# Denominator sums of blocks one to seven folded to one term on VectorE, and half of the first norm's transposes moved to DMA

## The chip, the cores and the metric

The kernel runs on one core of a Trainium2 chip. The metric is the device time of one execution in microseconds (us); lower is better. Before the change the median of three runs is 1134.34 us (1134.11 to 1134.49).

## What is computed

One transformer layer with conditioned norms: 2048 tokens of width 1024, multi-query attention with 32 heads of width 32 over one shared K and V, and a gated feed-forward network (FFN) of width 3584. All arrays are bf16.

```
mod = (silu(c) @ w_mod): sa, ca, ga, sb, cb, gb          # six rows of 1024
h = layernorm(x) * (1 + ca) + sa
q, k, v = h @ wq, h @ wk, h @ wv                          # 32 heads share k and v
p = softmax(q k^T / sqrt(32));  o = p v
x = x + ga * (o @ wo)
h = layernorm(x) * (1 + cb) + sb
out = x + gb * ((silu(h @ w1) * (h @ w3)) @ w2)
```

## The kernel before, in words

**Tiles.** Tokens are cut into 16 tiles of 128 and 8 blocks of 256. The first norm handles one token tile at a time (`lnt1`, L656): VectorE (DVE) computes statistics, GpSimd (POOL) the reciprocal root, and the normalized tile XN is made on ScalarE (ACT) for tiles 0 to 7 and on VectorE for tiles 8 to 15. XN has three slots, used in turn (tile number modulo 3: two halves of XNB and a piece of PS). TensorE (PE) then transposes the tile in eight 128x128 steps into a PSUM bank, and ACT or VectorE copies it into HT, the transposed activations. From HT come K (`k_proj`, L757, two token tiles a call, its result copied to KT by VectorE or ACT), V (`v_proj`, L772) and Q (`q_proj`, L787).

**Attention.** A unit is one block of 256 queries and four heads: 8 blocks times 8 groups make 64 units. A unit has 8 chunks of 256 keys, so there are 512 chunks in a fixed order. For a chunk, `s_exp` (L850) issues 8 score matmuls (named S<-QT,KT in the profile) and two exponentials on ACT, which write the chunk into one of ten slots of U. Chunk j of a unit needs KT of token tiles 2j and 2j+1. `av` (L881) multiplies the unit's 8 chunks by V on PE (64 matmuls, PB<-U,V) and forms the softmax denominators: VectorE adds chunks pairwise into slots of PS (`pairs`, L870, PS<-U), folds these slots further (PS<-PS), and PE sums what is left over the keys by multiplying with ones (PB<-PS,ONES, four matmuls per slot left). How far VectorE folds is `level(u)` (L878): for units 0 to 7 (block zero) level 2 leaves four slots, for later units level 3 leaves two. VectorE then inverts the denominators and scales the output into QT.

**The rest of a block.** `wo` (L946) applies the output projection, the second norm and its transposes (for blocks 1 to 6 by a DMA transpose issued from SyncE, SP; named QT<-XNB). `slab` (L1005) is the first half of the FFN, 14 slabs a block, each with a tanh on ACT; `quarter` (L1042) is the second half. The FFN of block n runs beside the attention of block n+1, so that of block 7 stands alone at the end. Weights stream from HBM through DMAs that SP issues.

**What sets the order.** All instructions are recorded as a graph; `Placer` (L187) places them one by one on the engines by planned durations, ready times and urgencies, and each engine then runs its list strictly in that order, waiting at semaphores. Score matmuls have the highest urgency; the other PE work fills the gaps. PLAN (L115) holds weights for every 16 chunks, which shift urgencies. All instructions are played through one helper, so that the profile gives L22 for nearly all of them, and tile names tell them apart. PE works in modes: score matmuls on row groups, full matrices, and column groups for values and denominators.

**The start.** SP issues the loads of x, of two slices of w_mod and of wq, then waits until the last part of wq has landed and issues WO and the first chunks of w_mod for the other fields (W2S<-in_w_mod; `mod_chunk`, L809).

Of the kernel before, what the change touches and what calls it, by code (L numbers as in the profile page):

```python
# [42 lines left out]
class Graph:  # L43
# [63 lines left out]
    def alias(self, new, old):  # L107
# [5 lines left out]


PLAN = [  # L115
    (0.2, 0.03, 0.0, 0, 1.4,
     {"q/pe": -9, "slab/act": -80, "wo/dve": -71, "ln/pe": -112, "ln/act": 31, "k/pe": 3, "k/dve": 33}),
    (0.0, 0.12, 0.2, 1, 0.2,
     {"av/pe": -2, "q/pe": -9, "pair/dve": -2, "av/dve": -33, "slab/act": -18, "ln/pe": -57, "ln/act": 23}),
    (0.0, 0.16, 0.02, 0, 0.7, {"wo/pe": 106, "q/pe": -45, "q/dve": -74, "ln/pe": -118, "ln/dve": 4, "mod/pe": -24}),  # L120
    (0.0, 0.16, 0.02, 0, 0.7, {"wo/pe": 106, "q/pe": -45, "q/dve": -74, "ln/pe": -118, "ln/dve": 4, "mod/pe": -24}),
    (0.2, 0.24, 0.2, 1, 0.6, {"q/pe": 47, "mc/pe": 46, "ln/act": -12, "k/pe": 22}),
    (0.0, 0.12, 0.2, 0, 1.8,
     {"wo/pe": -44, "quarter/pe": 47, "q/pe": 33, "mc/pe": 36, "pair/dve": -14, "wo/dve": -1, "ln/act": -12,
      "k/pe": 22}),
    (0.0, 0.11, 0.2, 1, 1.5, {"q/pe": 47, "mc/pe": 46, "av/dve": 6, "ln/act": -12, "k/pe": 22}),
    (0.0, 0.11, 0.2, 1, 1.9, {"q/pe": -13, "mc/pe": 46, "av/dve": 4, "ln/act": -12, "k/pe": 22}),
    (0.0, 0.11, 0.2, 0, 3.4, {"wo/pe": 35, "an/dve": 55, "slab/dve": 1}),
    (0.0, 0.11, 0.2, 1, 1.4, {"av/dve": -11, "an/dve": 55, "slab/dve": 1, "q/dve": 9}),
    (0.0, 0.11, 0.1, 0, 2.4,  # L130
     {"wo/pe": 14, "slab/pe": 12, "quarter/pe": 3, "q/pe": -6, "av/dve": 18, "an/dve": 69, "slab/act": -1,
      "quarter/dve": -7}),
    (0.0, 0.11, 0.05, 0, 2.4, {"slab/act": 6, "wo/dve": 53}),
    (0.0, 0.11, 0.2, 0, 2.9, {"wo/pe": 46, "an/dve": 55, "slab/dve": -89, "q/dve": 67}),
    (0.0, 0.11, 0.2, 1, 1.3, {"wo/pe": -13, "pair/dve": 6, "an/dve": 55, "slab/dve": -89, "q/dve": 67}),
    (0.0, 0.11, 0.1, 1, 2.7,
     {"slab/pe": -132, "q/pe": 47, "mc/pe": 46, "pair/dve": -13, "av/dve": 23, "slab/dve": -39, "slab/act": -20,
      "quarter/dve": -47, "ln/act": -12, "k/pe": 22}),
    (0.0, 0.11, 0.1, 1, 2.3,
     {"slab/pe": -132, "q/pe": 47, "mc/pe": 46, "pair/dve": -13, "av/dve": -84, "slab/act": -20,  # L140
      "quarter/dve": -47, "ln/act": -12, "k/pe": 22}),
    (0.0, 0.11, 0.2, 1, 4.1,
     {"wo/pe": 138, "slab/pe": -132, "quarter/pe": 13, "q/pe": 47, "mc/pe": 46, "pair/dve": -13, "av/dve": -83,
      "slab/dve": -39, "slab/act": -20, "quarter/dve": -47, "ln/act": -12, "k/pe": 22}),
    (0.0, 0.11, 0.2, 1, 1.3,
     {"slab/pe": -124, "q/pe": 47, "mc/pe": 46, "pair/dve": -24, "av/dve": -89, "an/dve": -26, "slab/dve": -39,
      "slab/act": -20, "ln/act": -12, "k/pe": 22}),
    (0.0, 0.11, 0.05, 1, 3.7,
     {"wo/pe": -5, "quarter/pe": 48, "pair/dve": -3, "av/dve": -2, "slab/act": -7, "wo/dve": 20}),
    (0.0, 0.11, 0.05, 1, 3.7,  # L150
     {"wo/pe": -5, "quarter/pe": 48, "pair/dve": -3, "av/dve": -2, "slab/act": -7, "wo/dve": 20}),
    (0.0, 0.11, 0.2, 1, 2.6,
     {"wo/pe": 112, "slab/pe": -124, "quarter/pe": 26, "q/pe": 20, "mc/pe": 46, "pair/dve": 13, "av/dve": -89,
      "an/dve": -26, "slab/dve": -39, "slab/act": -20, "quarter/dve": 35, "wo/dve": -2, "ln/act": -12,
      "k/pe": 22}),
    (0.0, 0.11, 0.2, 1, 1.3,
     {"slab/pe": -124, "quarter/pe": 26, "q/pe": 52, "mc/pe": 46, "pair/dve": 13, "av/dve": -72, "an/dve": -26,
      "slab/dve": -39, "slab/act": -20, "quarter/dve": 35, "wo/dve": -6, "ln/act": -12, "k/pe": 22}),
    (0.0, 0.11, 0.05, 1, 2.6,
     {"slab/pe": -124, "quarter/pe": 26, "q/pe": 20, "mc/pe": 46, "av/dve": -89, "slab/dve": -39,  # L160
      "slab/act": -20, "quarter/dve": 35, "ln/act": -12, "k/pe": 22}),
    (0.0, 0.11, 0.05, 1, 1.4,
     {"slab/pe": -124, "quarter/pe": 26, "q/pe": 20, "mc/pe": 5, "av/dve": -89, "slab/act": -20,
      "quarter/dve": 35, "ln/act": -12, "k/pe": 22}),
    (0.0, 0.11, 0.2, 0, 1.6, {"wo/pe": 74, "pair/dve": 40, "av/dve": -2, "an/dve": 55, "slab/dve": -102, "q/dve": 6}),
    (0.0, 0.11, 0.2, 1, 1.4, {"wo/pe": -13, "pair/dve": 40, "av/dve": -2, "an/dve": 55, "slab/dve": -88}),
    (0.0, 0.11, 0.05, 1, 1.9,
     {"slab/pe": -124, "quarter/pe": -21, "q/pe": 20, "mc/pe": 46, "pair/dve": 43, "av/dve": -89,
      "slab/dve": -39, "slab/act": -20, "quarter/dve": 35, "ln/act": -12, "k/pe": 22}),
    (0.0, 0.11, 0.05, 1, 1.9,  # L170
     {"slab/pe": -124, "quarter/pe": -21, "q/pe": 20, "mc/pe": 46, "pair/dve": 43, "av/dve": -89,
      "slab/act": -20, "quarter/dve": 35, "ln/act": -12, "k/pe": 22}),
    (0.0, 0.11, 0.2, 0, 3.4, {"wo/pe": 61, "q/pe": -20, "pair/dve": 3, "slab/dve": -23, "wo/dve": 33}),
    (0.0, 0.11, 0.2, 1, 1.4, {"wo/pe": -5, "quarter/pe": 48, "pair/dve": -20, "av/dve": -27, "slab/act": -7}),
    (0.0, 0.11, 0.05, 0, 2.1,
     {"slab/pe": -124, "quarter/pe": -21, "q/pe": 20, "mc/pe": 46, "pair/dve": 43, "av/dve": -89,
      "slab/dve": -39, "slab/act": -20, "quarter/dve": 35, "q/dve": -75, "ln/act": -12, "k/pe": 22}),
    (0.0, 0.11, 0.05, 0, 4.0,
     {"slab/pe": -124, "quarter/pe": -21, "q/pe": 20, "mc/pe": 46, "pair/dve": 43, "av/dve": -89,
      "slab/act": -20, "quarter/dve": 35, "q/dve": -75, "ln/act": -12, "k/pe": 22}),  # L180
    (0.0, 0.11, 0.2, 0, 3.7,
     {"wo/pe": -4, "slab/pe": -43, "q/pe": 20, "mc/pe": 46, "pair/dve": 43, "av/dve": 55, "slab/dve": -39,
      "slab/act": -20, "quarter/dve": 35, "q/dve": -75, "ln/act": -12, "k/pe": 22}),
]


class Placer:  # L187
# [121 lines left out]
    def commit(self, n, e, k, start):  # L309
        eng, fn, dur = n.alts[k]  # L310
        e = eng
        s = n.sess
        if s is not None and s.bank is None:
            bt, b = self.bank_for(n)
            s.bank = b
            s.prev = self.bank_of[b][1]
            self.bank_of[b] = None
            for p in s.prev:
                n.preds.setdefault(p, False)
        n.eng = e  # L320
        if e == "sp" or n.dma is not None:
            self.t[e] = start + dur
            self.bw = max(self.bw, start + 2.6) + n.nbytes / n.bw
            n.fin = self.bw + 0.5
        else:
            if e == "dve" and n.tag in ("pair", "av"):
                self.lock = start + dur
            if e == "pool" and self.lock > start:
                dur = max(dur, self.lock - start + (0.43 if dur > 0.5 else 0.1))
            self.t[e] = start + dur  # L330
            n.fin = start + dur + n.post + self.SEM
        if e == "pe":
            if s is not None and n.mode == "F":
                s.fill = any(not x.done and x is not n and x.alts[0][0] == "pe" for x in s.nodes)
                if s.fill:
                    self.fills.add(s)
                else:
                    self.fills.discard(s)
            if n.mode == "S":
                self.step += 1  # L340
            self.mode = n.mode
            if n.mode != "S":
                self.run_of = n.mode
            else:
                self.t_s = self.t["pe"]
        n.done = True
        if s is not None:
            s.left -= 1
            if s.left == 0:
                users = [x for x in s.nodes if x.eng != "pe"] or [s.nodes[-1]]  # L350
                self.bank_of[s.bank] = (max(x.fin for x in users), tuple(users))
        self.emit(n, e, fn)
        self.free_pending()
# [90 lines left out]
def build(nc, x_in, wq_in, wk_in, wv_in, wo_in, w1_in, w3_in, w2_in, c_in, wmod_in, out, S, D, F):  # L444
# [89 lines left out]
    def xkey(tt):  # L534
        return [("X", tt // 2, tt % 2, q) for q in range(4)] if tt < 6 else [("XS", tt)]
# [120 lines left out]
    def lnt1(tt, vt):  # L656
# [10 lines left out]
               reads=xkey(tt) + [("RS", tt), ("NB", tt)], writes=[("XN", slot)], vt=vt)  # L667
        else:
            ln_norm(xap, tt, xkey(tt), slot, vt)
        static = tt < 6  # L670
        s = None if static else Sess()
        bk = [("S", tt)] if static else [("sess", id(s), tt)]
# [203 lines left out]
           writes=[("PS", (c + k) % NP) for k in range(2)], vt=c + 101.0, post=0.08)  # L876

    def level(u):  # L878
        return 2 if u < 8 else 3

    def av(u):  # L881
        G.tag = "av"
# [342 lines left out]
```

## Time and profile before

| what | value |
|---|---|
| median of the runs | 1134.34 us |
| the profiled execution's own time | 1134.47 us |
| its span (first to last instruction) | 1132.6 us |
| PE busy | 1113.1 us (98%) |
| ACT busy | 1026.0 us (91%) |
| DVE busy | 951.9 us (84%) |
| DMA, mean over the span | 185 GB/s |
| clock granted to PE | 1.00 |
| first score matmul | 30.13 us |
| last score matmul | 1033.80 us |

Times in the trace are microseconds from the start of the span; what lies around the span is 1.9 us of the execution's own time. A matmul's end is modelled, so a busy PE is not PE at its peak. An engine's busy time is the union of its instructions. In the lines of waits the engine that waits stands to the left of the arrow.

### The profile page before, as it was taken

The numbers are of one execution on the slowest core, as the hardware profiler recorded it, in microseconds if no ns is written. First come the engines' busy times: TensorE is split into PE (matmuls) and PEld (weight loads), VectorE is DVE, ScalarE is ACT, GpSimd is POOL, SyncE is SP. The second block draws the span as 40 slices with busy tenths as digits, with TensorE's granted clock in tenths as the row PEclk, the third lists the DMA queues.
The fourth block names the chain that finished last, engine by engine and source line by source line (L and its number), as shares of the span: only waits on it lengthen the run. The fifth ranks groups of instructions, "written<-read, shape, count | busy, mean of one in ns | idle before, by whom it ended". The sixth has DMA issues, their size and how long they took to land.

```text
span 1132.6 us, 34805 instructions
## 1 busy us (share of the span) xinstructions
PE 1113.1 (98%) x15600; PEld 754.6 (67%) x15600; DVE 951.9 (84%) x1544; ACT 1026.0 (91%) x1165; POOL 53.8 (5%) x95
## 2 busy tenths in 40 slices
PE   7999999999999999999999999999999999999998
PEld 6643546666577656776567756776577657766887
DVE  7888899989988888888988998888988988888442
ACT  6999999999999999999999999999999999996110
POOL 5100000000100001000100000000100000000000
PEclk9999999999999999999999999999999999999999
DMA  9500379665596667766596658765696559667793
GB/s 344 184 2 1 114 225 242 186 196 151 129 263 194 173 166 209 208 191 165 141 262 192 174 148 237 196 193 142 173 248 195 160 146 238 190 185 209 217 296 116
DMA packets 374292, 209.47 MB, mean 185 GB/s; under 512 B 17536, under 2 KB 365952, under 8 KB 374144
## 3 DMA queue, kind: packets, MB, share of 16 engines
q1 hardware_dynamic: 373712, 207.11, 65.8%
q8 instruction: 123, 2.02, 0.8%
q14 instruction: 25, 0.20, 0.1%
q10 hardware_dynamic: 432, 0.13, 0.0%
HBM read 199.89 MB, written 4.19 MB: 180 GB/s over the span
## 4 chain that ended last, share of the span: by engine, by line
PE 63%; ACT 31%; DVE 4%; DMA 1%; issue 0%; POOL 0%; SPq 0%; DVEq 0%
PE PB L22 47%; ACT U L22 30%; PE S L22 16%; DVE PS L22 2%; DMA W<-in_A_wq_dram 1%; ACT HT L22 1%; DVE HT L22 1%; DVE RB L22 0%; SPq L22 0%; DVE ST L22 0%; DVE W L22 0%; ACT XNB L22 0%; POOL PS L22 0%; DVE XNB L22 0%; POOL RS L22 0%
## 5 line engine op out<-in xcount | busy, mean ns | idle before, releaser
L22 ACT ACTIVATE U<-S 128x1024 bf16<-128x1024 f32 x1024 | 964.3, 1111 | 9.0 <-PE S L22 8.8
L22 DVE TENSOR_TENSOR PS<-U 128x2048 bf16<-128x2048 bf16 x256 | 309.7, 1214 | 11.7 <-ACT U L22 10.3
L22 DVE TENSOR_TENSOR PS<-PS 128x1024 bf16<-128x1024 bf16 x368 | 249.5, 684 | 4.7
L22 PE MATMUL PB<-QT,W 128*128 128x256 bf16 x1856 | 229.6, 273 | 0.0
L22 PE MATMUL S<-QT,KT 32*128 32x256 bf16 x4096 | 203.5, 273 | 6.0 <-ACT U L22 4.0
L22 PEld LDWEIGHTS PB<-QT,W 128*128 128x128 bf16 x1856 | 170.3, 98 | 46.6 <-issue 28.3
L22 PE MATMUL PB<-W2S,HT 128*128 128x256 bf16 x1512 | 189.1, 273 | 0.0
L22 PEld LDWEIGHTS PB<-W2S,HT 128*128 128x128 bf16 x1512 | 137.5, 98 | 42.4 <-issue 26.4
L22 PEld LDWEIGHTS S<-QT,KT 32*128 32x128 bf16 x4096 | 60.8, 92 | 132.7 <-ACT U L22 118.7
L22 PE MATMUL PB<-U,V 128*32 128x256 bf16 x4032 | 123.5, 273 | 0.0
L22 PE MATMUL PB<-QT,HT 128*128 128x256 bf16 x960 | 119.9, 273 | 0.0
L22 PEld LDWEIGHTS PB<-U,V 128*32 128x32 bf16 x4032 | 100.8, 97 | 18.8 <-issue 7.0
L22 ACT ACTIVATE HT<-PB 128x512 bf16<-128x512 f32 (+1 forms) x110 | 77.6, 707 | 32.0 <-PE PB L22 31.8
L22 PEld LDWEIGHTS PB<-QT,HT 128*128 128x128 bf16 x960 | 88.2, 98 | 23.7 <-issue 14.1
L22 PE MATMUL PB<-HT,W 128*128 128x256 bf16 (+1 forms) x576 | 101.8, 318 | 1.0 <-DVE HT L22 0.6
L22 DVE SCALAR_TENSOR_TENSOR HT<-HT,PB 128x512 bf16<-128x512 bf16 x102 | 69.4, 681 | 34.2 <-ACT HT L22 33.4
L22 DVE TENSOR_TENSOR HT<-HT,PB 128x512 bf16<-128x512 bf16 x102 | 69.5, 681 | 19.2 <-PE PB L22 18.5
L22 PEld LDWEIGHTS PB<-HT,W 128*128 128x128 bf16 x576 | 49.9, 97 | 38.1 <-issue 15.2
L22 DVE STREAM_TRANSPOSE RB<-PB 128x256 f32<-128x256 f32 x63 | 28.2, 448 | 38.7 <-PE PB L22 38.5
L22 PE MATMUL PB<-WO,QT 128*128 128x512 bf16 x232 | 57.3, 381 | 0.0
L22 POOL TENSOR_SCALAR RS<-MV 128x1 f32<-128x1 f32 x32 | 10.5, 329 | 969.9 <-DVE MV L22 966.9
L22 ACT ACTIVATE HT<-S 128x512 bf16<-128x512 f32 (+1 forms) x15 | 10.9, 736 | 30.5 <-PE S L22 30.5
(115 smaller groups left out, 675.2 us busy)
## 6 DMA issues: line engine op xcount, KB each, us to landing
W<-in_B_w_dram SPq DMA_DIRECT2D x150, 512.0 KB, 4.8
W2S<-in_B_w_dram SPq DMA_DIRECT2D x28, 1792.0 KB, 8.6
HT<-in_B_w_dram SPq DMA_DIRECT2D x74, 512.0 KB, 4.8
W2S<-in_w_mod_dram SPq DMA_DIRECT2D x8, 1024.0 KB, 7.2
X<-in_A_x_dram SPq DMA_DIRECT2D x8, 512.0 KB, 7.0
out_dram<-X SPq DMA_DIRECT2D x7, 512.0 KB, 9.1
U<-in_B_w_dram SPq DMA_DIRECT2D x1, 3584.0 KB, 13.5
W2S<-in_B_w_dram SPq DMA_DIRECT2D x1, 3584.0 KB, 15.2
```

What stands on the lines that cost most here:

```text
L22: return getattr(e, call[0])(*call[1], **call[2])
```

## The change

Three edits. `level(u)` becomes 4 for units 8 to 63: VectorE adds the last two slots of a unit as well, and PE multiplies one slot by ones in place of two. For token tiles 8 to 15 the first norm's transposition becomes a DMA transpose from XN to HT, issued by SP; its eight PE transposes and the copy out of PSUM go. The planner is given a duration of its own for these transposes, which doesn't pass through its queue of DMA bytes. And PLAN is replaced as a whole, so that the order changes on every engine.

```
-        return 2 if u < 8 else 3
+        return 2 if u < 8 else 4
...
         else:
             ln_norm(xap, tt, xkey(tt), slot, vt)
+        if tt >= 8:
+            o = op("sp", lambda: [lambda e: e.dma_start_transpose(HT[:, :, tt * P:(tt + 1) * P], XN[slot])], 0.5,
+                   reads=[("XN", slot)], writes=[("HT", cc, tt) for cc in range(NC)], vt=vt, dma=("HTL", slot), nbytes=1 << 18)
+            o.bw = -262144.0 / 1.0 * 1.0
+            return
         static = tt < 6
...
-            self.bw = max(self.bw, start + 2.6) + n.nbytes / n.bw
-            n.fin = self.bw + 0.5
+            if n.bw < 0:
+                n.fin = start + 2.6 - n.nbytes / n.bw + 0.5
+            else:
+                self.bw = max(self.bw, start + 2.6) + n.nbytes / n.bw
+                n.fin = self.bw + 0.5
...
-    (0.2, 0.03, 0.0, 0, 1.4,
-     {"q/pe": -9, "slab/act": -80, "wo/dve": -71, "ln/pe": -112, "ln/act": 31, "k/pe": 3, "k/dve": 33}),
...
+    (0.0, 0.12, 0.2, 0, 2.6,
+     {"slab/pe": -44, "q/pe": -9, "mc/pe": 25, "slab/dve": -38, "slab/act": -18, "wo/dve": -95, "ln/pe": -112,
+      "ln/act": 172, "k/dve": 33, "mod/pe": 109}),
...
```

In the built program the matmuls with ones fall from 576 to 352. On SP the transposes of tiles 8, 9 and 10 stand behind the last load of x; then come the two loads of WO, the transpose of tile 11, two loads of w_mod chunks, and the transposes of tiles 12 to 15. On VectorE the norm of tile 11 waits until the transpose of tile 8 has freed its slot, that of tile 12 waits for the transpose of tile 9, and that of tile 15 for that of tile 12. On PE the K projections of token tiles 8 to 15 (four calls of `k_proj`) stand ahead of score groups 2, 3, 6 and 7 in the list and wait for the transposes.

More of the change, by code (lines that the diff above doesn't have):

```diff
@@ L115 @@
 PLAN = [
-    (0.2, 0.03, 0.0, 0, 1.4,
-     {"q/pe": -9, "slab/act": -80, "wo/dve": -71, "ln/pe": -112, "ln/act": 31, "k/pe": 3, "k/dve": 33}),
[L118 to L121, printed above, removed]
@@ L122 @@
-    (0.2, 0.24, 0.2, 1, 0.6, {"q/pe": 47, "mc/pe": 46, "ln/act": -12, "k/pe": 22}),
-    (0.0, 0.12, 0.2, 0, 1.8,
-     {"wo/pe": -44, "quarter/pe": 47, "q/pe": 33, "mc/pe": 36, "pair/dve": -14, "wo/dve": -1, "ln/act": -12,
-      "k/pe": 22}),
-    (0.0, 0.11, 0.2, 1, 1.5, {"q/pe": 47, "mc/pe": 46, "av/dve": 6, "ln/act": -12, "k/pe": 22}),
-    (0.0, 0.11, 0.2, 1, 1.9, {"q/pe": -13, "mc/pe": 46, "av/dve": 4, "ln/act": -12, "k/pe": 22}),
-    (0.0, 0.11, 0.2, 0, 3.4, {"wo/pe": 35, "an/dve": 55, "slab/dve": 1}),
@@ L129 @@
[L129 to L139, printed above, removed]
+    (0.0, 0.12, 0.2, 0, 2.6,
+     {"slab/pe": -44, "q/pe": -9, "mc/pe": 25, "slab/dve": -38, "slab/act": -18, "wo/dve": -95, "ln/pe": -112,
+      "ln/act": 172, "k/dve": 33, "mod/pe": 109}),
+    (0.0, 0.15, 0.2, 1, 0.7,
+     {"wo/pe": 16, "slab/pe": -44, "q/pe": -17, "mc/pe": 25, "pair/dve": 8, "slab/dve": -38, "slab/act": -18,
+      "wo/dve": -95, "ln/pe": -112, "ln/dve": -122, "ln/act": 172, "k/dve": 33, "mod/pe": 109, "kb/pe": 8}),
@@ new lines @@
+    (0.0, 0.15, 0.1, 0, 0.7, {"wo/pe": 106, "q/pe": -78, "q/dve": -74, "ln/pe": -118, "ln/dve": 4, "mod/pe": -24}),
+    (0.2, 0.17, 0.1, 0, 0.8, {"mc/pe": 22, "av/dve": 1, "an/dve": -68, "q/dve": -18, "k/dve": 75, "kb/pe": 16}),
+    (0.0, 0.23, 0.2, 0, 1.3,
+     {"quarter/pe": -49, "mc/pe": 22, "av/dve": 106, "slab/dve": 9, "quarter/dve": 26, "q/dve": -28,
+      "kb/pe": -47}),
+    (0.0, 0.13, 0.2, 1, 3.3,
+     {"av/pe": -14, "wo/pe": -44, "quarter/pe": -31, "q/pe": 28, "mc/pe": -6, "pair/dve": -2, "an/dve": -18,
+      "wo/dve": 2, "q/dve": 16, "ln/act": -12, "k/pe": 22}),
@@ new lines @@
+    (0.0, 0.14, 0.2, 1, 3.3,
+     {"av/pe": -14, "wo/pe": -44, "quarter/pe": 47, "q/pe": 28, "pair/dve": -2, "an/dve": -18, "wo/dve": 2,
+      "q/dve": 16, "ln/act": -12, "k/pe": 22}),
+    (0.0, 0.11, 0.2, 1, 3.8,
+     {"av/pe": 11, "wo/pe": -44, "quarter/pe": 47, "pair/dve": -49, "av/dve": -48, "wo/dve": 2, "ln/act": -12,
+      "k/pe": 22}),
+    (0.0, 0.16, 0.2, 1, 0.5,
+     {"av/pe": 11, "wo/pe": -44, "quarter/pe": 47, "pair/dve": -2, "av/dve": -48, "an/dve": -9, "wo/dve": 2,
+      "q/dve": -59, "ln/act": -12, "k/pe": 22}),
@@ new lines @@
+    (0.0, 0.16, 0.2, 1, 0.5,
+     {"av/pe": 11, "wo/pe": -44, "quarter/pe": 47, "pair/dve": -2, "av/dve": -48, "an/dve": -9, "wo/dve": 2,
+      "q/dve": -59, "ln/act": -12, "k/pe": 22}),
+    (0.0, 0.11, 0.2, 0, 1.1, {"wo/pe": -17, "slab/dve": -19, "wo/dve": 53}),
+    (0.0, 0.11, 0.2, 1, 1.6, {"q/pe": -13, "mc/pe": 46, "av/dve": 40, "ln/act": -12, "k/pe": 22}),
+    (0.0, 0.12, 0.2, 0, 0.7,
+     {"slab/pe": -25, "quarter/pe": 11, "q/pe": -15, "mc/pe": -14, "av/dve": 40, "ln/act": -12, "k/pe": 22}),
@@ new lines @@
+    (0.0, 0.11, 0.2, 1, 1.5, {"av/dve": -8, "an/dve": 29, "slab/act": 6, "wo/dve": 53}),
+    (0.0, 0.11, 0.2, 1, 1.5, {"av/dve": -8, "an/dve": 29, "slab/act": 6, "wo/dve": 53}),
+    (0.0, 0.11, 0.2, 1, 1.5, {"av/dve": -8, "an/dve": 29, "slab/act": 6, "wo/dve": 53}),
+    (0.0, 0.11, 0.2, 1, 1.5, {"av/dve": -8, "an/dve": 29, "slab/act": 6, "wo/dve": 53}),
+    (0.0, 0.11, 0.2, 1, 1.5, {"av/dve": -8, "an/dve": 29, "slab/act": 6, "wo/dve": 53}),
+    (0.0, 0.11, 0.2, 0, 1.4,
+     {"mc/pe": 46, "av/dve": 35, "slab/dve": -88, "slab/act": 7, "q/dve": -25, "ln/act": -12, "k/pe": 22}),
@@ L140 @@
+    (0.0, 0.11, 0.2, 0, 1.4,
+     {"mc/pe": 46, "av/dve": 35, "slab/dve": -88, "slab/act": 7, "q/dve": -25, "ln/act": -12, "k/pe": 22}),
+    (0.0, 0.11, 0.2, 1, 2.3,
      {"slab/pe": -132, "q/pe": 47, "mc/pe": 46, "pair/dve": -13, "av/dve": -84, "slab/act": -20,
       "quarter/dve": -47, "ln/act": -12, "k/pe": 22}),
-    (0.0, 0.11, 0.2, 1, 4.1,
-     {"wo/pe": 138, "slab/pe": -132, "quarter/pe": 13, "q/pe": 47, "mc/pe": 46, "pair/dve": -13, "av/dve": -83,
-      "slab/dve": -39, "slab/act": -20, "quarter/dve": -47, "ln/act": -12, "k/pe": 22}),
@@ L145 @@
[L145 to L180, printed above, removed]
@@ L181 @@
-    (0.0, 0.11, 0.2, 0, 3.7,
-     {"wo/pe": -4, "slab/pe": -43, "q/pe": 20, "mc/pe": 46, "pair/dve": 43, "av/dve": 55, "slab/dve": -39,
-      "slab/act": -20, "quarter/dve": 35, "q/dve": -75, "ln/act": -12, "k/pe": 22}),
+    (0.0, 0.11, 0.2, 1, 1.4,
+     {"slab/pe": -132, "quarter/pe": 13, "q/pe": 47, "mc/pe": 46, "av/dve": 3, "slab/dve": -39,
+      "quarter/dve": -47, "wo/dve": -48, "q/dve": -7, "ln/act": -12, "k/pe": 22}),
+    (0.0, 0.11, 0.2, 1, 1.4,
+     {"slab/pe": -132, "quarter/pe": 13, "q/pe": 47, "mc/pe": 46, "av/dve": 3, "slab/dve": -39,
+      "quarter/dve": -47, "wo/dve": -48, "q/dve": -7, "ln/act": -12, "k/pe": 22}),
@@ new lines @@
+    (0.0, 0.11, 0.2, 1, 1.4,
+     {"slab/pe": -132, "quarter/pe": 13, "q/pe": 47, "mc/pe": 46, "av/dve": 3, "slab/dve": -39,
+      "quarter/dve": -47, "wo/dve": -48, "q/dve": -7, "ln/act": -12, "k/pe": 22}),
+    (0.0, 0.11, 0.2, 1, 1.4,
+     {"slab/pe": -132, "quarter/pe": 13, "q/pe": 47, "mc/pe": 46, "av/dve": 3, "slab/dve": -39,
+      "quarter/dve": -47, "wo/dve": -48, "q/dve": -7, "ln/act": -12, "k/pe": 22}),
+    (0.0, 0.11, 0.2, 1, 1.4,
+     {"slab/pe": -132, "quarter/pe": 13, "q/pe": 47, "mc/pe": 46, "av/dve": 3, "slab/dve": -39,
+      "quarter/dve": -47, "wo/dve": -48, "q/dve": -7, "ln/act": -12, "k/pe": 22}),
@@ new lines @@
+    (0.0, 0.11, 0.2, 1, 1.4,
+     {"slab/pe": -132, "quarter/pe": 13, "q/pe": 47, "mc/pe": 46, "av/dve": 3, "slab/dve": -39,
+      "quarter/dve": -47, "wo/dve": -48, "q/dve": -7, "ln/act": -12, "k/pe": 22}),
+    (0.0, 0.11, 0.2, 1, 1.4,
+     {"slab/pe": -132, "quarter/pe": 13, "q/pe": 47, "mc/pe": 46, "av/dve": 3, "slab/dve": -39,
+      "quarter/dve": -47, "wo/dve": -48, "q/dve": -7, "ln/act": -12, "k/pe": 22}),
+    (0.0, 0.11, 0.2, 1, 1.4,
+     {"slab/pe": -132, "quarter/pe": 13, "q/pe": 47, "mc/pe": 46, "av/dve": 3, "slab/dve": -39,
+      "quarter/dve": -47, "wo/dve": -48, "q/dve": -7, "ln/act": -12, "k/pe": 22}),
@@ new lines @@
+    (0.0, 0.11, 0.2, 1, 1.4,
+     {"slab/pe": -132, "quarter/pe": 13, "q/pe": 47, "mc/pe": 46, "av/dve": 3, "slab/dve": -39,
+      "quarter/dve": -47, "wo/dve": -48, "q/dve": -7, "ln/act": -12, "k/pe": 22}),
+    (0.0, 0.11, 0.2, 1, 1.4,
+     {"slab/pe": -132, "quarter/pe": 13, "q/pe": 47, "mc/pe": 46, "av/dve": 3, "slab/dve": -39,
+      "quarter/dve": -47, "wo/dve": -48, "q/dve": -7, "ln/act": -12, "k/pe": 22}),
+    (0.0, 0.11, 0.2, 0, 4.0,
+     {"av/pe": 6, "slab/pe": -43, "q/pe": 20, "mc/pe": 56, "pair/dve": -56, "slab/act": 23, "quarter/dve": 61,
+      "wo/dve": 5, "q/dve": -75, "ln/act": -12, "k/pe": 22}),
@@ L184 @@
+    (0.0, 0.11, 0.2, 0, 4.0,
+     {"av/pe": 6, "slab/pe": -43, "q/pe": 20, "mc/pe": 56, "pair/dve": -56, "slab/act": 23, "quarter/dve": 61,
+      "wo/dve": 5, "q/dve": -75, "ln/act": -12, "k/pe": 22}),
 ]
```

## The prediction

> **What bounds the kernel now.** I read the page's busy times, then one window per block of 64 score groups, then the waits, then the start in the timeline and the DMA answers.
>
> ```profile
> core 0: us, PE busy (x) PEld busy (x) DVE busy (x) ACT busy (x) POOL busy (x), PEclk, DMA share, GB/s
> 30.13:153.09 122.96, 119.93 (x1793) 60.89 (x1792) 107.18 (x185) 122.71 (x136) 3.69 (x8) 1.00 0.24 81
> 153.09:282.33 129.24, 124.89 (x1906) 83.32 (x1907) 117.26 (x190) 127.53 (x145) 2.55 (x4) 1.00 0.74 201
> 282.33:408.48 126.15, 125.70 (x1796) 85.56 (x1793) 112.27 (x176) 124.78 (x142) 4.95 (x6) 1.00 0.70 189
> 1033.80:1132.60 98.80, 95.86 (x911) 82.28 (x910) 41.87 (x74) 11.06 (x17) 1.59 (x4) 1.00 0.80 221
> ```
>
> The first number after a window is its length. Block zero (first row) is ACT's: 128 exponentials of 0.917 us each (30 in 27.70 us, less the last one's longer end) are 117.4 us, and ACT idles 0.25 us. Blocks 2 to 6 take 126.15 us each. There ACT needs 117.4 us and 14 tanhs that push the next exponential back by 0.48 us (6.7 us), together 124.1 us; PE is full. So PE bounds them, with ACT 2.05 us behind. Block 1 has VectorE busy 91%, and its chain rests on VectorE's PS sums for 13%. The last row is the tail, the FFN of block 7, bound by PE.
>
> ```profile
> PEld S L22 <- ACT U L22: 118.7, 440, 1.1
> ACT U L22 <- PE S L22: 8.8, 8, 1.4
> ```
>
> PE waits for exponentials often but 0.27 us at a time, most of which is its 0.21 us pause at any change of mode; ACT hardly waits for PE. Both are nearly full: what is taken from PE in blocks 1 to 7 is worth its size up to 2.05 us a block, and what delays ACT's stream at the start is paid in full.
>
> **Denominators.**
>
> ```profile
> L22 DVE TENSOR_TENSOR PS<-PS 128x1024 bf16<-128x1024 bf16 x368 | 249.5, 684 | 4.7
> L22 PE MATMUL PB<-PS,ONES 128*32 128x256 bf16 x568 | 27.5, 277 | 0.2 <-DVE PS L22 0.2
> ```
>
> A run of 64 value matmuls, of the same column-group form, fills 1.86 us, so four take 0.11 us. One group of four goes per unit: 0.87 us per block, 6.1 us over 56 units. The mode change stays. VectorE gains 56 sums; in a run they start 0.61 us apart, so 34 us in all, 4.9 us a block. Blocks 2 to 7 then have VectorE at (112.3 + 4.9) / 125.4 = 93%. I cost this at nothing there, since the 0.61 us lie between the last pair and a matmul that PE reaches after filler work; without that cover VectorE's lateness could eat the whole 0.87 us.
>
> **Order.** Counting the built order by blocks: blocks 2 and 3 hold 14 and 22 full-width (256-column) matmuls fewer, the tail 18 more. FFN matmuls go through PE at 0.109 us. A score group and 12 of them recur every 1.74 us: 0.22 + 1.31 leaves 0.105 us for each of two mode changes. Blocks 2 to 7 had 137 changes each; now 147, 136 and four times 138. Block 2: -0.87 - 1.5 + 1.05 = -1.3 us. Block 3: -0.87 - 2.4 - 0.1 = -3.4, of which ACT's floor lets -2.0 through. Blocks 4 to 7: four times -0.77, -3.1. Sum **-6.4 us** (ends: 0 if VectorE takes it all, -12.3 if all six blocks fall to ACT's floor). Block 1: -0.8 us of matmuls; but VectorE is on the chain for some 28 us between 184 and 234, about two units' worth, so +1.2: **+0.4** (ends -0.8, and +4.9 if all eight sums show). Tail: 18 x 0.109 = **+2.0** (ends 0, where these matmuls fill waits, and +2.0); its own extra sum lies beside FFN matmuls.
>
> **The start.** Sixteen ACT or VectorE copies shrink to eight. Before, ACT squeezes five copies of 0.91 us between its exponentials:
>
> ```profile
> 45.09 1.04 ACT L22 ACTIVATE HT<-PB 128x1024 bf16<-128x1024 bf16 x1
> 46.01 1.96 ACT L22 ACTIVATE U<-S 128x1024 bf16<-128x1024 f32 x2
> 47.82 0.51 ACT L22 ACTIVATE KT<-PB,QKB 128x256 bf16<-128x256 f32 x1
> 48.17 12.07 ACT L22 ACTIVATE U<-S 128x1024 bf16<-128x1024 f32 x13
> ```
>
> Thirteen exponentials precede 48.17, so chunk 7 starts at 49.09, and from there ACT never idles in block zero. The new order gives ACT three more KT copies (0.37 us each). If the transposes came in time, chunk 7 would start 5 x 0.91 - 1.1 = 3.5 us earlier. Do they?
>
> ```profile
> W2S<-in_A_x_dram SPq DMA_DIRECT2D x1, 1024.0 KB, 16.0
> WO<-in_A_wo_dram SPq DMA_DIRECT2D x2, 1024.0 KB, 6.8
> W2S<-in_w_mod_dram SPq DMA_DIRECT2D x2, 1024.0 KB, 11.8
> QT<-XNB SPq DMA_TRANSPOSE x12, 3.1
> ```
>
> The last number is the time from issue to landing. The second norm's transposes land after 3.1 us, with their queue nearly empty. The last load of x, same queue, needs 16.0 us behind the others. In the 40 slices of 30 to 33 us and of one idle-queue transpose (297 to 302 us):
>
> ```profile
> DMA  9989658639301222343525494526989989989999
> DMA  0000000199999999971000000000000200000600
> ```
>
> the loads run dry, unevenly, between 30.3 and 32.5 (I take 31.3), and a transpose fills the engines for ten slices of 0.125 us: 1.25 us. In line, the tiles go thus. Tiles 8 to 10 are normalized by 28.9 and done at 31.3 + 3.75 = 35.0. WO and the two w_mod loads took 11.5 us before (32.2 to 43.7), 5.75 a pair: WO to 40.8, tile 11 to 42.0, w_mod to 47.8, tiles 12 to 14 to 51.5, tile 15 to 52.8. Tile 15's norm needs tile 12's slot (landed 49.5), which still lets its issue (1.2 us before data flow) reach the queue by 51.4. Landing follows the data by 0.45 us: 53.25. Then PE's eight K matmuls 1.05, KT copy 0.47, scores 0.40, handovers 0.4: chunk 7 at 55.55, **+6.5 us**. PE runs in order, so the K projection of tiles 10 and 11 also holds score groups 3 to 5 from about 39 to 43, and VectorE's wait for tile 8 holds a QT and a KT copy; both end before chunk 7 and cost nothing on top. Eight transposes also take 8 x 1.24 us of SP, which idles there. Ends: -3.5 (each lands in 3.1 us), and +9 (slowest DMA engine, 2 us later, counts).
>
> The Trainium skill, "DMA: Bandwidth & Descriptors", section "Queues, rings and completion order", says that SP has one ring on each DMA engine and that descriptors are consumed in ring order; the 16.0 us against 3.1 agree, and no trace of before shows a transpose behind loads. By that rule the sum is the one above; without it, that of the first rival. The same page's "Latency and other measured facts" gives a DMA transpose 261 GB/s; the trace has 256 KB in 1.25 us, 210 GB/s, and I keep the trace.
>
> **Sum.** +6.5 + 0.4 - 6.4 + 2.0 = +2.5 us, against the profiled execution's own 1134.47 us (span 1132.6 and 1.9 around it; the median is 0.13 lower): **1137.0 us**.
>
> **Rivals.**
> - *The transposes overtake the loads* and land within some 3.1 us. Then K is never late: -3.5 + 0.4 - 6.4 + 2.0 = -7.5 us, **1127.0**. For it: 12 of 12 transposes did so before. Against it: none had loads in front. It decides from where tile 15 lands before 46.8 (2.3 us ahead of 49.09). Chance 0.20.
> - *Transposes cheaper in a queue*: loads move 375 GB/s, so 256 KB might take 0.7 us; eight of them save 4.4 us. Start +2.1, together -1.9: **1132.6**. For it: a lone transpose may not fill the engines. Against: their share reads 9 in tenths. Chance 0.16.
> - *VectorE becomes the bound.* Nothing is gained in blocks 2 to 7 and block 1 pays +3.3: 6.5 + 3.3 + 2.0 = +11.8, less about 2 for the shifted matmuls: **1144**. For it: 91% in block 1 already, and 93% from there on. Against: waits of PE for VectorE are 0.2 to 0.4 us now. Chance 0.12.
> - *The change doing nothing* is excluded by the built order: 352 matmuls with ones for 576.
>
> **How the numbers follow.** Forecast 1137.0, chance 0.52, itself spread some 3 us either way. This measurement can tell 0.2% (2.3 us) from no change: faster lies below 1132.1, slower above 1136.7. Of the forecast I put 0.38 above 1136.7 and 0.14 between; the second rival gives 0.12 same and 0.04 faster. Slower 0.38 + 0.12 = 0.50, same 0.26, faster 0.24. The range 1128.5 to 1142.5 leaves out about half of the first rival and most of the third.
>
> **What would show it.** Transposes of tiles 11 to 15 landing well over 3.1 us after issue; gaps on ACT near 39 to 43 and 50 to 55; chunk 7 near 55.5; blocks 4 to 7 at 125.4 us; PS<-PS 424 times. Wrong if the transposes land within 4 us, if a steady block stays at 126 us or more, or if VectorE's idle time vanishes in blocks 1 to 7.

## The result, and the profile after

| | before | after |
|---|---|---|
| median | 1134.41 us (1134.11 to 1134.67) | 1149.59 us (1148.73 to 1150.06) |
| ratio | | 1.0133, interval 1.0115 to 1.0151 |
| span of the profiled execution | 1132.6 us | 1147.2 us |
| granted clock of PE | 1.00 | 0.993 |

The change costs 15.2 us; 1137.0 us had been forecast, with 1142.5 as the upper end. To see where it went, the starts of equal score groups are compared. The first unit's last group starts at 60.20 us instead of 48.47, group 64 at 165.06 instead of 153.09, the last one (511) at 1045.85 instead of 1033.80. So the span's 14.6 us are 12.0 up to group 64, 0.1 over blocks 1 to 7 together, and 2.5 in the tail.

The windows below answer those of before, with the same columns: block 0, block 1, block 2, block 4, tail. A window runs from one score group to the same place 64 groups later.

```profile
30.20:165.06 134.86, 119.58 (x1783) 61.26 (x1801) 108.91 (x186) 120.22 (x134) 3.28 (x9) 0.94 0.34 94
165.06:289.25 124.19, 120.67 (x1749) 79.69 (x1749) 116.96 (x191) 124.15 (x143) 1.58 (x4) 1.00 0.73 201
289.25:415.44 126.19, 125.16 (x1744) 82.87 (x1748) 116.69 (x183) 124.62 (x143) 3.35 (x6) 1.00 0.67 184
540.75:667.52 126.77, 125.53 (x1760) 84.92 (x1762) 116.82 (x183) 125.01 (x143) 5.04 (x6) 1.00 0.69 188
1045.85:1147.20 101.35, 97.95 (x923) 83.91 (x924) 43.31 (x77) 11.06 (x17) 1.59 (x4) 1.00 0.79 221
```

Before, block 1 takes 125.64 us and each of blocks 2 to 6 126.15. (The prediction's window of 129.24 us for block 1 held 65 score groups; the row after it, of 64 groups, is right.) Block 1 became 1.45 us shorter, block 2 is unchanged, block 3 is 0.8 shorter, and blocks 4 to 7 are each 0.5 to 0.6 us longer. PE's busy time in block 4 barely moved (125.72 before, 125.53 now), VectorE's grew by 5.6 us (4.9 foreseen), and ACT's idle time grew.

The start shows the largest loss. First the timeline of PE after the change, then the windows with the granted clock in the third column from the end:

```profile
37.06 1.66 PE L22 MATMUL PB<-SAB,W 128*128 128x64 bf16 x48
44.25 1.89 PE L22 MATMUL PB<-HT,PS 128*128 128x256 bf16 x8 [5.52 <-DMA HT<-PS]
...
53.74 1.86 PE L22 MATMUL PB<-HT,PS 128*128 128x256 bf16 x8 [1.66 <-DMA HT<-XNB]
...
56.94 1.83 PE L22 MATMUL PB<-SCC,W2S 128*128 128x64 bf16 x32
58.60 1.03 PE L22 MATMUL PB<-HT,PS 128*128 128x256 bf16 x8
...
60.20 0.40 PE L22 MATMUL S<-QT,KT 32*128 32x256 bf16 x8
```

```profile
38.00:44.00 6.00, 0.72 (x24) 0.60 (x20) 2.73 (x6) 1.14 (x2) 1.54 (x4) 0.79 1.07 324
44.00:50.00 6.00, 3.80 (x40) 1.74 (x40) 1.76 (x6) 3.74 (x5) 0.79 (x2) 0.50 1.10 341
50.00:56.00 6.00, 4.34 (x101) 3.55 (x94) 2.71 (x7) 2.70 (x4) 0.00 (x0) 0.50 1.00 161
```

PE waits 5.52 us for tile 11's transpose and 1.66 us for tile 13's. From 44 to 56 us its clock is 0.50: the same eight K matmuls take 1.89 and 1.86 us there, and 1.03 us once the clock is back. ACT meanwhile waits up to 7.0 us for a K.

### The profile page after: what moved, and what is told of

It reads as the page before. It is cut to its first block, busy times and chain, and to the rows that moved or that the text cites. A ratio compares the mean times of both kernels' runs of the same rounds, so it can differ in the third digit from the quotient of the medians.

```text
span 1147.2 us, 34233 instructions
## 1 busy us (share of the span) xinstructions
PE 1110.7 (97%) x15279; PEld 748.9 (65%) x15312; DVE 988.4 (86%) x1593; ACT 1023.9 (89%) x1163; POOL 51.0 (4%) x96
## 3 DMA queue, kind: packets, MB, share of 16 engines
q8 instruction: 120, 1.97, 0.7%
## 4 chain that ended last, share of the span: by engine, by line
ACT 50%; PE 43%; DVE 3%; DMA 2%; issue 1%; POOL 0%; POOLq 0%; DVEq 0%
ACT U L22 47%; PE PB L22 29%; PE S L22 14%; ACT HT L22 3%; DVE PS L22 2%; DMA HT<-PS 1%; DMA HT<-XNB 1%; DVE ST L22 0%; DVE QT L22 0%; DVE HT L22 0%; DVE RB L22 0%; ACT XNB L22 0%; ACT PS L22 0%; DVE MV L22 0%; DVE RC L22 0%
## 5 line engine op out<-in xcount | busy, mean ns | idle before, releaser
L22 ACT ACTIVATE U<-S 128x1024 bf16<-128x1024 f32 x1024 | 962.5, 1120 | 10.8 <-PE S L22 8.3
L22 DVE TENSOR_TENSOR PS<-PS 128x1024 bf16<-128x1024 bf16 x424 | 286.6, 686 | 4.6
L22 PE MATMUL PB<-QT,W 128*128 128x256 bf16 x1824 | 226.3, 273 | 2.0 <-DVE HT L22 1.0
L22 PEld LDWEIGHTS PB<-QT,W 128*128 128x128 bf16 x1824 | 165.7, 98 | 50.2 <-issue 25.9
L22 PE MATMUL PB<-W2S,HT 128*128 128x256 bf16 x1540 | 194.2, 273 | 0.0
L22 PE MATMUL PB<-QT,HT 128*128 128x256 bf16 x928 | 116.1, 273 | 0.4
L22 PE MATMUL PB<-HT,W 128*128 128x256 bf16 (+1 forms) x558 | 97.9, 316 | 3.6 <-issue 1.7
L22 PEld LDWEIGHTS PB<-QT,HT 128*128 128x128 bf16 x928 | 84.6, 98 | 24.8 <-issue 14.1
L22 ACT ACTIVATE HT<-PB 128x512 bf16<-128x512 f32 (+1 forms) x102 | 68.6, 672 | 8.7 <-PE PB L22 8.7
L22 POOL TENSOR_SCALAR RS<-MV 128x1 f32<-128x1 f32 x32 | 14.6, 456 | 983.7 <-DVE MV L22 978.6
L22 PE MATMUL PB<-WO,QT 128*128 128x512 bf16 x210 | 52.1, 380 | 1.6 <-issue 1.1
```

What stands on the lines that cost most here:

```text
L22: return getattr(e, call[0])(*call[1], **call[2])
```

## The experiments

Twelve kernels ran. "Order held" means that each engine's list of instructions stays as it was but for the edit. Of those that compute all of the reference, none beats before. The last column is block 4 (from score group 256 to group 320), read as the steady block. The other blocks from 2 to 6 are within 0.1 us of it in before and the h_mm and h_av4 runs; in h_av12 they take 125.41 us, in a_av12 124.9 to 125.4, in f_lvl4 125.0 to 133.1; in after, a_nosum and the s_ runs blocks 4 to 6 are alike.

| run | median, us | ratio to before, interval | first unit's last group, us | block 4, us |
|---|---|---|---|---|
| before | 1134.41 | 1 | 48.47 | 126.15 |
| after | 1149.59 | 1.0115 to 1.0151 | 60.20 | 126.77 |
| h_mm | 1133.73 | 0.9982 to 1.0001 | 48.29 | 126.09 |
| h_av4 | 1131.00 | 0.9953 to 0.9979 | 48.78 | 125.62 |
| h_av12 | 1129.54 | 0.9941 to 0.9974 | 48.69 | 125.54 |
| a_av12 | 1141.52 | 1.0046 to 1.0076 | 60.77 | 125.32 |
| h_lvl4 | 1156.27 | 1.0172 to 1.0202 | 48.67 | 129.28 |
| h_thin | 1136.31 | 1.0005 to 1.0024 | 48.12 | 126.42 |
| f_lvl4 | 1174.27 | 1.0335 to 1.0370 | 48.34 | 133.10 |
| a_nosum | 1149.27 | 1.0111 to 1.0141 | 60.78 | 126.77 |
| s_wo | 1143.74 | 1.0064 to 1.0094 | 54.01 | 126.76 |
| s_late | 1144.76 | 1.0067 to 1.0102 | 55.90 | 126.76 |
| s_pool | 1151.51 | 1.0134 to 1.0164 | 62.94 | 126.77 |
| s_warm | 1152.71 | 1.0143 to 1.0173 | 63.79 | 126.76 |

### What the saved matmuls are worth: h_mm, h_av4, h_av12, a_av12

**h_mm**: before, order held, fewer matmuls with ones.

```
+                kk = ks[:1] if lev == 3 else ks
...
-                    stop=(k == slots[-1]), tile_position=(0, 32 * h), skip_group_check=True)
-                    for k in ks for h in range(4)]
+                    stop=(k == (kk[-1] if lev == 3 else slots[-1])), tile_position=(0, 32 * h), skip_group_check=True)
+                    for k in kk for h in range(4)]
```

> The order of before is held; from unit 8 on one slot instead of two is multiplied by ones and nothing is added on VectorE, so half of the denominators' terms of these units are left out. It prices the removed matmuls alone. Theory 1 (PE bounds the blocks): four matmuls a unit for 56 units at 0.109 us save 6.1 us, about 1128.3. Theory 2 (VectorE is the bound): the same 1128.3, because VectorE has no more to do, and the difference to the run with the added sum is VectorE's price. Theory 3 (ACT's floor): within 2 us of before.

Measured: 1133.73 us, 0.7 us under before, and a steady block of 126.09 us: theory 3. PE as a whole is not the bound. The window of that block, and what PE's weight loads, which come first, waited for most in it:

```profile
530.43:656.52 126.09, 125.17 (x1758) 85.47 (x1762) 111.39 (x175) 124.73 (x143) 4.98 (x6) 1.00 0.69 189
```

```profile
PEld S L22 <- ACT U L22: 15.1, 57, 0.5
```

Before, this wait came to 14.3 us in the same block. Of the 0.87 us of matmuls that went, 0.8 came back as waiting for exponentials. So in the intervals with these matmuls ACT's stream sets the pace. It idles little, yet more than the idle column of the profile tells: an exponential is recorded with 1.11 us but, back to back, they start 0.904 us apart, so a late start of up to 0.2 us shows no idle time at all. Reading the start of every exponential and tanh of this block in before one by one gives 128 x 0.904 + 14 x 0.475 = 122.4 us and 3.8 us of late starts. Of these, 3.4 lie at seven of the block's eight runs of value matmuls: 1.64 at the first, where twelve FFN matmuls share the interval with the run, and 0.29 to 0.30 at the others. The timeline of PE in before shows one of them:

```profile
580.49 0.40 PE L22 MATMUL S<-QT,KT 32*128 32x256 bf16 x8
580.82 1.93 PE L22 MATMUL PB<-U,V 128*32 128x256 bf16 x64
582.68 0.40 PE L22 MATMUL S<-QT,KT 32*128 32x256 bf16 x8
...
592.85 0.40 PE L22 MATMUL PB<-PS,ONES 128*32 128x256 bf16 x8
```

A run of 64 value matmuls sets two score groups 2.19 us apart, where two exponentials last 1.81; ACT starts 0.29 us late there. The matmuls with ones stand in another interval, in which PE waits for ACT anyway. That made a new theory, to be tested with value matmuls.

**h_av4** and **h_av12**: before, order held, 4 or 12 of the 64 value matmuls of a unit left out (`q == NJ - 1` below is h_av4; h_av12 has `q >= NJ - 3`).

```
-            def mm(b, q=q):
+            def mm(b, q=q, nk=1 if u >= 8 and q == NJ - 1 else 2):
...
-                    start=(q == 0 and kk == 0), stop=(q == NJ - 1 and kk == 1), tile_position=(0, 32 * h),
-                    skip_group_check=True) for kk in range(2) for h in range(4)]
+                    start=(q == 0 and kk == 0), stop=(q == NJ - 1 and kk == nk - 1), tile_position=(0, 32 * h),
+                    skip_group_check=True) for kk in range(nk) for h in range(4)]
```

> The kernel before, with 60 instead of 64 value matmuls in a unit from unit 8 on (one key tile's values in sixteen are left out): the same 0.11 us of TensorE a unit that the earlier run took from the denominators for 0.9 us in all, taken this time from the run of value matmuls between two score groups. New theory (ACT sets the pace, and that run of 64 opens a gap of 0.29 us on ACT once a unit): each unit shortens by 0.11 us, blocks 1 to 7 by about 0.85 us each, the whole to about 1128.5. Theory of the prediction (PE is full, any matmul counts) gives the same here, but it had to give it for the denominators too. Theory 3 (ACT's floor lies at 126 us a block): within 2 us of before, as with the denominators.

> The kernel before, with 52 instead of 64 value matmuls in a unit from unit 8 on (three key tiles' values in sixteen are left out): 0.35 us a unit, a little more than the gap of 0.29 us that the run of 64 opens on ACT. Theory (ACT sets the pace; its gaps lie at these runs): the gaps fall to 0.1 us or less, a block from 126.15 to about 124.1, the whole to about 1120. If the gaps have another cause, they stay at 0.29 and the whole within 4 us of before.

Measured: 1131.00 us with 4 left out, a block of 125.62 us; 1129.54 us with 12, a block of 125.41 (block 4: 125.54). The same four matmuls a unit are worth 3.4 us in the value run and 0.7 among the denominators, so the place matters as the theory says, though only half of 0.11 us a unit came through (the late start fell from 0.29 to 0.24 in most units). Where it fell short is h_av12: 0.35 us a unit, some 2.8 us a block, gave 0.6 to 0.7, where 2 us a block and 1120 us in all had been expected. The late start of 0.29 is gone in most units, but starts of 0.04 to 0.14 us late appear at several other exponentials, and a unit in the FFN's part takes 16.14 us instead of 16.19. At some of them PE waits for ACT as well: an interval with twelve FFN matmuls grew from 1.75 us to 1.81 and 1.83, one with sixteen from 2.19 to 2.32. What spaces these, the hand-over from exponential to score group and back or something else, was not tried. Shown is that blocks 2 to 6, fed in this order, came no lower than 125.4 us with 2.8 us less on PE.

**a_av12**: after, with the same 12 matmuls left out.

> The changed kernel with the same 12 value matmuls a unit left out. If the 0.6 us that its blocks 4 to 7 take more than those of before sit at the same runs of value matmuls (gaps of 0.08 and 0.37 us for 0.29), the two kernels' blocks become equal within 0.2 us, near 124.2, and the whole falls by some 17 us, to about 1132. If the planned order loses elsewhere (or on VectorE), the difference of 0.6 us a block stays.

Measured: 1141.52 us, about half of the fall that had been expected; the block 125.32 us against 125.54 in h_av12. The 0.6 us that after's steady blocks take more is gone. The starts of the exponentials say where it sat: block 4 of after has 0.6 us more of late starts than that of before, and 0.5 of it lies at the value runs and the score groups just ahead of them. The timeline of PE in after shows the new order there:

```profile
587.58 1.05 PE L22 MATMUL PB<-QT,HT 128*128 128x256 bf16 x8
588.55 1.25 PE L22 MATMUL PB<-QT,W 128*128 128x256 bf16 x10
589.74 0.40 PE L22 MATMUL S<-QT,KT 32*128 32x256 bf16 x8
590.07 1.93 PE L22 MATMUL PB<-U,V 128*32 128x256 bf16 x64
591.93 0.40 PE L22 MATMUL S<-QT,KT 32*128 32x256 bf16 x8
```

Eighteen FFN matmuls now stand in the interval ahead of the run. The score group at 589.74 is itself 0.08 us late for ACT, and the one after the run 0.36: 0.44 for 0.29.

### What VectorE's added sum costs: h_lvl4, h_thin, a_nosum, f_lvl4

**h_lvl4**: before, order held, the whole edit of the denominators; the added sum follows the last one that before has, after a wait for its own engine to finish that one; PE's matmuls are those of h_mm.

```
+                    two = lev == 3 and k0 == 4 and w == 2
-                    op("dve", lambda k0=k0, k1=k1: [lambda e: e.tensor_tensor(PS[:, k0], PS[:, k0], PS[:, k1], ALU.add)],
+                    o = op("dve", lambda k0=k0, k1=k1, two=two: [lambda e: e.tensor_tensor(
+                        PS[:, k0], PS[:, k0], PS[:, k1], ALU.add)] + ([lambda e: e.tensor_tensor(
+                            PS[:, 0], PS[:, 0], PS[:, 4], ALU.add)] if two else []),
...
```

> The order of before is held on every engine; only the denominators change: from unit 8 on VectorE adds one more sum a unit, and one slot instead of two is multiplied by ones. Theory 1 (the sums cost VectorE nothing that PE notices; the written plan lost the gain in the changed kernel): blocks 2 to 7 fall from 126.15 to about 125.3 us each, the whole is 5 to 6 us under before, about 1128.5. Theory 2 (VectorE becomes the bound, the third rival of the prediction): no block shrinks, 1134 or more. Theory 3 (ACT's floor lies higher than 124.1 us a block, so a shorter PE list only moves the waits): within 2 us of before.

**h_thin**: the same with `PS[:, 0, :, 0:32]` in place of `PS[:, 0]`, a sum of 0.22 us instead of 0.69; place and wait stay.

> The run with the order of before and one more sum a unit (1156 us), with that sum cut to 32 of its 256 columns, as in the run of the changed kernel with the cut sum (the denominators are incomplete by what is left out). Its place, its wait and the matmuls stay. If the sum's length on VectorE costs the 22 us there (0.71 us a unit between two sums with work of other kinds behind it, which PE then waits for): with some 0.25 us a unit left, about a third of it stays, 1137 to 1143. If the place costs it (PE's matmul with ones now waits for one more step, whatever its length): 1150 or more.

Measured: 1156.27 us and 1136.31 us. My theory 1 was wrong for this order: the sum costs 22 us, and with a third of its length 1.8, where some 7 had been expected. So what costs is its length, far more than its place or its wait. The waits of PE for VectorE in h_lvl4, over the whole span:

```profile
PE PB L22 <- DVE HT L22: 16.6, 35, 1.0
PEld PB L22 <- DVE PS L22: 15.6, 23, 1.4
PEld PB L22 <- DVE HT L22: 14.9, 40, 0.8
PE PB L22 <- DVE PS L22: 10.5, 18, 1.1
```

Together 57.6 us; before has 12.4 in the same four rows, h_thin 21.6. VectorE runs its list in order, so behind the added sum the products HT that the FFN's matmuls need come late too (the first and third row). Idle 11% of a block, VectorE still has no 0.7 us to spare at that place.

**a_nosum**: after, order held, the last sum of a unit cut to 32 of 256 columns.

> The changed kernel, with the last sum of each unit cut to 32 of its 256 columns (the denominators of blocks one to seven are incomplete by what is left out), so VectorE has some 0.4 us a unit less to do and the order is held. Theory 1 (the written plan's order costs blocks 4 to 7): they stay at 126.7 us each and the whole at 1148 to 1150. Theory 2 (VectorE's added sums cost it): blocks 4 to 7 fall to about 125.4 us and the whole to about 1143.

Measured: 1149.27 us, VectorE busy 113.6 instead of 116.8 us in a block that takes the same 126.77 us, and block 1 the same 124.20. In the new order the part of the sums that went is hidden. That the new PLAN was made to keep room for them is not shown.

**f_lvl4**: before's PLAN, only `level(u)` changed, the order worked out anew.

> The plan of before and PE's transposes for all tiles; the denominators added down to one term a unit, and the order worked out anew by the planner, which puts the added sums where it has room (with the order held and the sum put in behind the last pair's the time rose by 22 us). Theory 1 (the sums cost nothing where the order has room; ACT's pace hides the matmuls saved): blocks 2 to 7 at 126 to 126.5 us, the whole within 3 us of before, 1132 to 1137. The prediction's theory (PE bound): 1128.5. Rival (VectorE the bound): above 1140.

Measured: 1174.27 us. The first two theories missed; the rival's "above 1140" came, but the run doesn't show that it came by VectorE. In block 4 ACT waits for PE's FFN sums ahead of a tanh or an exponential (ACT U <- PE PB 4.1 us, ACT HT <- PE PB 2.5 us), where before has none of that. PE's waits for VectorE grew as well: over the span the four rows above come to 25.7 us. With a slightly different graph the same PLAN made an order far worse than both kernels, and in it the sums can't be told from the order.

### The start: s_wo, s_late, s_pool, s_warm

**s_wo** and **s_late**: after, only SP's list changed. In s_wo the two WO loads go behind the last transpose, in s_late the two w_mod loads as well.

```
+    sp = pl.ops["sp"]
+    last = max(i for i, r in enumerate(sp) if r.node.dma[0] == "HTL")
+    wo_l = [r for r in sp[:last] if r.node.dma[0] == "WO"]
+    pl.ops["sp"] = [r for r in sp[:last + 1] if r not in wo_l] + wo_l + sp[last + 1:]
```

> The changed kernel with only the two WO loads moved on SP's queue, behind the last transpose; the two loads of w_mod stay ahead of tile 12's transpose. Theory of the queue: tile 11 lands some 6 us earlier, near 38 us, PE's wait of 5.5 us for it goes and the clock stays up there, the last score group of the first unit comes at 51 to 54 instead of 60.2, the whole at 1141 to 1144. Theory 2 (slots and landing set it): within 2 us of 1149.

> The changed kernel, with the eight transposes issued ahead of the two WO and the two w_mod loads on SP's queue. Theory 1 (the transposes are late because they stand behind these loads in the queue): the landings of tiles 11 to 15 come 9 to 10 us earlier, the first unit's last score group starts near 51 instead of 60.2, the whole is about 1140. Theory 2 (transposes are late by themselves: they wait for their slots and for each other): the last score group stays within 2 us of 60.2 and the whole within 2 us of 1149. If the gate matrices become late instead, the tanh of the first adaptive norm shows it, later in the first block.

Measured: the last group of the first unit at 54.01 us in s_wo (1143.74 us) and 55.90 in s_late (1144.76 us). The transposes come as soon as there are no loads ahead: the five from XNB land 3.1 us after their issue in s_late (median), 6.6 in after. In s_late tile 15 is there before 47 us, yet the last group is not near the 51 us that were expected, for another input is late now. SP and PE in s_late:

```profile
43.81 1.28 SPq L22 DMA_TRANSPOSE HT<-XNB  x1
45.14 1.36 SPq L22 DMA_DIRECT2D W2S<-in_w_mod_dram  x2
...
51.73 1.89 PE L22 MATMUL PB<-SCC,W2S 128*128 128x64 bf16 x32 [3.55 <-DMA W2S<-in_w_mod_dram]
53.43 1.90 PE L22 MATMUL PB<-HT,PS 128*128 128x256 bf16 x8
...
55.90 0.61 PE L22 MATMUL S<-QT,KT 32*128 32x256 bf16 x8
```

PE's list has 32 matmuls with w_mod ahead of the last K projection, so here PE waits for w_mod where it waited for the transposes before.

**s_pool**: after, WO and the first w_mod loads issued by POOL, whose DMAs go through a queue of their own.

```
+        if n.dma is not None and n.dma[0] in ("WO", "WMB") and self.step < 8 and any(k[0][0] == "HTL" for k in self.dma_sem):
+            e = "pool"
         known = self.known[e]
```

> The changed kernel with the WO loads and the first loads of w_mod of the start issued by POOL on its own queue instead of SP's; every engine's other work is held. It tells a queue's order from the DMA engines' share. If the transposes wait behind loads only because they stand in the same queue: they land 3 to 4.5 us after their issue although the loads run at the same time, tile 15 before 48 us, PE's wait of 5.5 us goes, the last score group of the first unit comes at 50 to 53, the whole at 1139.5 to 1143. If what counts is that 16 DMA engines are full, whatever the queue: landings stay at 6 us and more, the last score group at 57 or later, the whole within 3 us of 1149.3.

Measured: 62.94 us, 1151.51 us, worse than after. The issues of POOL and SP, and what PE waited for:

```profile
30.88 1.77 POOL L22 DMA_DIRECT2D WO<-in_A_wo_dram  x2
32.64 1.77 POOL L22 DMA_DIRECT2D W2S<-in_w_mod_dram  x2
34.66 9.97 SPq L22 DMA_TRANSPOSE HT<-PS  x1
49.35 1.89 PE L22 MATMUL PB<-HT,PS 128*128 128x256 bf16 x8 [7.17 <-DMA HT<-PS]
```

Tile 11's transpose has no load ahead of it in its own queue and still needs 14.6 us, the one before it, tile 10's, 15.9; both come when the four loads (4 MB) are through. So with these loads in flight another queue was no way past them. The packets tell why. The page counts 8448 more packets under 512 B in after than in before, 1056 for each of the eight transposes. POOL's queue moved 5.24 MB in 1360 packets, 1088 for these four loads. Between 40 and 46 us the two queues (q0 is POOL's, q1 SP's) moved:

```profile
q0 software_dynamic: 514, 1.97, 94.5%
q1 hardware_dynamic: 514, 0.13, 11.3%
```

Equal numbers of packets, and 15 times the bytes in POOL's: the queues take turns packet by packet, so that a transpose of 1056 small packets lasts about as long as 1056 of the large ones. The Trainium skill, "DMA: Bandwidth & Descriptors", section "Queues, rings and completion order", has each DMA engine go round the queues in turn, a packet at a time. Its packet is a batch of several descriptors, and whether the profile counts the same thing is not shown; the equal counts agree with taking turns. Other sizes of packet were not tried.

**s_warm**: after, with 76 matmuls on the identity ahead of the K projections that wait.

> The changed kernel with extra matmuls on the identity (76 in all, their results are not used) ahead of the four K projections that wait for a transpose, so TensorE works through its 5.5 us wait; loads and transposes as they are. If the granted clock of 0.50 between 44 and 56 us, that follows the wait, is part of the loss: the clock stays above 0.9 there, the last score group of the first unit comes 2 to 4 us earlier than 60.2, the whole at 1145.5 to 1147.5. If the loads alone set it (the clock is a symptom): the last score group within 1 us of 60.2, the whole within 1.5 us of 1149.3.

Measured: 63.79 us, 1152.71 us. The run doesn't settle what it was made for. The clock stayed at 1.00 from 38 to 50 us and the eight K matmuls at 45.80 took 1.05 us; but tile 11 landed 1.6 us later, the clock fell to 0.71 in the window after 50 us all the same, and 20 of the extra matmuls, at half speed, took 4.45 us on the way to the last group. The clock's part in after is therefore only bounded by durations: from 53.74 us on K took 1.86 us for 1.03, a score group 0.61 for 0.40, the w_mod matmuls 1.83 for the 1.17 they take in s_wo; 1.7 us together. Which of the waits brought the clock down there is open.

## Why the prediction was wrong

- **"PE bounds them, with ACT 2.05 us behind": failed.** It is the step that loses most: -6.4 us were forecast for blocks 2 to 7 and +1.5 came. Two busy shares near 100% do not say who sets the pace. With 0.87 us a block taken from PE alone, h_mm gained 0.06; with some 2.8 taken in h_av12, 0.6 to 0.7. ACT's floor was put at 124.1 us, from 0.917 us an exponential; back to back they start 0.904 us apart, 122.4 us a block, and the other 3.8 us are late starts. In this order blocks 2 to 6 came no lower than 125.4. ACT's late starts lie nearly all at the value runs (3.4 of 3.8 us), and the saved matmuls don't stand there.
- **Order, 0.109 us for each full-width matmul moved: failed** for the same reason. Blocks 4 to 7 were to gain 0.77 us each and lost 0.5 to 0.6, most of it at the value runs (a_av12).
- **VectorE at nothing: right for after, for another reason than given.** a_nosum shows no cost. But the cover is the new order, not filler work as such: at before's places the sum costs 22 us. The rival of 1144 comes nearest to the measured time by luck: after doesn't show its mechanism, h_lvl4 does.
- **Block 1, +0.4: too high.** It gained 1.45 us; the 1.2 us put down for VectorE there did not come.
- **The start, +6.5: right in kind, +11.7 to 12.0 in size.** Loads delay the transposes (s_wo, s_late), so the first rival, overtaking, is out. The second, cheaper transposes, was partly right: behind loads or other transposes they moved at some 290 GB/s, 0.9 us each and not 1.25 (the rates from 49.8 us on, below). It did not help, for two terms were too small. The first is the landings: tile 15 came at 55.2 us for 53.25, and tile 13 was awaited until 53.74, where the sum has it at 50.7. The loads of WO were issued at 33.63 us instead of 30.23, behind two transposes whose issue held SP for 3.9 and 3.5 us, and landed at 43.25, 2 us later than summed. Tile 13 landed 2.5 us after tile 12, though it and the next were issued: the engines nearly stood still in between, as the rates in after from 48 to 56 us show, 0.2 us a number. Why is open. The second is the last stretch, in the next point.

```profile
GB/s 358 353 338 353 338 348 353 353 256 292 292 291 269 291 292 292 360 230 180 15 0 8 9 9 12 271 170 291 272 288 291 293 285 111 0 0 0 0 0 0
```

- **The last stretch, 2.3 us between tile 15 and the last group's exponential:** it took 5.4 (55.2 to 60.65). The sum has only tile 15's K there, but in PE's list tile 13's K projection, a score group, 32 w_mod matmuls and V's matmuls stand ahead of the last group, most of them at half clock. With WO out of the way s_wo took back 6.2 of the 11.7 us; no run took back the rest.
- **Waits of PE before chunk 7 that "cost nothing on top": failed as far as the clock goes.** While PE waited for tiles 11 and 13 its clock fell, by the estimate above up to 1.7 us. Which wait did it is open: with the first one filled, in s_warm, the clock fell after 50 us all the same.
- **The tail, +2.0:** 2.5 measured.

The sum as forecast was 6.5 + 0.4 - 6.4 + 2.0; it came as 12.0 - 1.4 + 1.5 + 2.5 = 14.6.

## What to carry to other kernels

When two engines are both near full, ask which intervals between two hand-overs are longer than the other engine's work in them; here work taken out of them was worth up to half its duration, and work taken out elsewhere next to nothing. Start-to-start distances find them where recorded durations overlap and hide idle time. A planned order belongs to one graph: the same edit was free in one order and cost 22 us in another. A transfer that replaces work at the start has to be counted against every load in flight, whatever its queue (s_pool), and the work that waits for it against everything that stands ahead of it in its engine's list.

## What the runs showed of the hardware

- PE's granted clock fell after waits of about 2 us. In s_wo the K matmuls after a wait of 2.01 us at 34.35 us ran at half speed (16 in 3.53 us), and the clock was 0.54 from 44 to 50 us with no wait over 1.9 us. The length of one wait does not decide it: after 1.82 us, in after at 34.38 us, eight K matmuls ran at full speed (1.05 us). The Trainium skill, "TensorE: Matmul & The Clock Gate", section "Part 1: The HAM clock gate", has the clock halved after an idle window of about 3.4 us; a single such gap was not needed here.
- SP was held longer by the issue of a transpose while the engines were full: 3.9 us in after and 9.97 us in s_pool, 1.23 us with nothing in flight (s_late). Whatever stands behind it in SP's list is issued later too.
- Two DMA queues shared the engines by packets and not by bytes: 514 packets each, 1.97 and 0.13 MB (s_pool, 40 to 46 us). A 256 KB transpose issued beside 4 MB of loads from the other queue took 14.6 us, beside nothing 3.1.
- Transposes that follow each other in the queue ran at some 290 GB/s (after, 49.8 to 51 us), one alone at some 210 (before, 298 to 299 us). Twice in after, from 34.4 and from 51.8 us, the engines moved 15 GB/s or less for 1.0 and 1.2 us with transposes issued.
